# A softmax division that is placed later in the plan and held there

## The chip, the core and the metric

The kernel runs on one core of a Trainium2 chip. The metric is the device time of one execution in microseconds (us). The core has TensorE for matrix products (PE in the rows, PEld for its weight loads), VectorE (DVE), ScalarE (ACT), GpSimd (POOL) and SyncE (SP), which here only issues transfers. Each engine works through its own queue of instructions in order, and an instruction that waits holds those behind it.

## What is computed

Attention over 4 batches of 8 heads, 576 tokens and a head size of 64, with a decay from the running sum of log f and a causal mask. A gated MLP with a spatial mixing over tokens follows, and then a second MLP with a token shift.

```python
scores = scale * np.matmul(q, k.transpose(0, 1, 3, 2))
decay = cum[:, :, :, None] - cum[:, :, None, :]
scores = np.where(causal, -1000000000.0, scores + decay)
attn = np.exp(scores - np.max(scores, axis=-1, keepdims=True))
attn = attn / (np.sum(attn, axis=-1, keepdims=True) + 1e-09)
x = np.matmul(attn, v)               # then heads side by side: 576 x 512 per batch
h = np.maximum(x @ w_in, 0.0)        # u, v: its two halves; v normalized per token
gated = u * (np.einsum('ts,bsd->btd', w_spatial, v_n) + b_spatial[None, :, None])
x = gated @ w_out
k = np.maximum(xk @ w_k, 0.0)        # xk, xr: mixes of x and x one token earlier
out = sigmoid(xr @ w_r) * (k * k @ w_v)
```

## The kernel before

The 32 heads are taken in 16 pairs. Each head passes the same steps. q and k of a pair are scaled, split into two 16-bit halves on ScalarE and VectorE (`qkhi`, `qklo`), and turned by a transposing transfer. `score` and `rowmax` find the row maxima (tile nm); `mrow` splits them (nmh), turns them with a product and sends them through DRAM (md) into the rows of qA. `scoreT` computes the transposed scores and their exponentials e on ScalarE, `causal` masks e on POOL, and `pv` multiplies with v, which has a block of ones beside it, so that the sums of the softmax come out as rows of the same PSUM tile o. There is one such tile.

The division follows. `head` (L359) copies o to xo, which has three buffers, and sends the head's row of sums to DRAM (rd<-xo, L368). Once per pair, `recip` (L370) fetches both rows spread over 128 partitions (r<-rd, L375), adds the small constant, scales and inverts them on VectorE (L376, L377), sends them back (rd<-r, L378) and fetches them spread over 64 partitions for each head (sr<-rd, L381, two transfers). `norm` (L383) multiplies xo by sr on POOL, 64 partitions at a time, which gives x. `xhi` (L390) copies x to the high 16-bit half of xt on ScalarE, and `xlo` (L393) computes the low half on POOL. All these transfers are issued by SyncE, as are the loads of q, k and v, the transposing transfers, and those of md and qA.

The MLP of a batch starts with xt of its four pairs: `m1v` and `m1u` are the products with w_in, `ln1` to `ln4` the normalization (with short scalar steps on POOL, mv), `m2` the spatial product. Its pieces lie between the heads of the next batch, and those of the last batch behind the last head. The second MLP comes after that.

The order of all this is a written plan. Every step has a due time in units of heads: the dictionary `P` holds offsets from a head's number g or, for pairs, from 2p, and `plan_attention` (L611) adds each step with its time and a priority. `run` (L605) sorts by time and then by priority and calls the steps, which gives the program order. The framework's scheduler then orders each engine's instructions anew: by its own reckoning of times it takes the instruction that is ready, the earlier one in program order first. So an instruction can pass others on its engine that the scheduler takes to be still waiting. `pin` (L56) calls `keep_in_program_order`, which puts an instruction behind the one before it on the same engine in program order; the others remain free.

Due times that matter for the change, as offsets from the head or pair: transposed scores at 0 to 0.66 and masks 0.06 later, products with v at 1.0 and 1.3, `head` at 1.35, `mrow` at 2p - 0.65, halves of k and q at 2p - 4.25 and 2p - 3.95, copies into kA and qA at 2p - 3.6 and 2p - 3.5, the MLP of batch b from 8b + 10.7 over 7 heads.

Of the kernel before, what the change touches and what calls it, by code (L numbers as in the profile page):

```python
# [7 lines left out]
F32 = mybir.dt.float32  # L8
# [5 lines left out]
ALU = mybir.AluOpType  # L14
# [14 lines left out]


P = dict(load=-8.0, sq=-5.6, ss=-5.2, sc=-5.0, hik=-4.6, lok=-4.25, hiq=-4.2, loq=-3.95, aux=-3.6,
         s=-2.4, m=-0.65, t=0.0, pv=1.0, out=1.35, rc=1.4, nr=1.9, xs=2.2, xl=2.4, mlp=2.7, mlplen=7.0, vload=-5.0, vsq=-3.0,
         w1=-3.8, w0=1.0, wsp=4.6)


# [4 lines left out]
class K:  # L40
# [318 lines left out]
    def head(self, g):  # L359

        nc = self.nc
        o = self.o.pop(g)
        h = g % 2
        t = self.xo[h] = self.at.tile([128, 576], F32, tag="xo", bufs=3, name="xo")
        nc.scalar.copy(t, o[:, 256:832])
        if h == 0:
            self.rd = [self.hl.tile([2, 576], F32, tag=f"rd{i}", bufs=2, name=f"rd{i}") for i in range(2)]
        nc.sync.dma_start(self.rd[0][h:h + 1], t[64 - 64 * h:65 - 64 * h])  # L368

    def recip(self, p):  # L370

        nc = self.nc
        sv = self.sv[p // 4]
        r = self.at.tile([128, 9], F32, tag="r9", bufs=2, name="r9")
        nc.sync.dma_start(r, self.rd[0].rearrange("h (p c) -> (h p) c", c=9))  # L375
        nc.vector.tensor_scalar(r, r, 1e-9, sv[:, 1:2], op0=ALU.add, op1=ALU.mult)  # L376
        nc.vector.reciprocal(r, r)  # L377
        nc.sync.dma_start(self.rd[1].rearrange("h (p c) -> (h p) c", c=9), r)  # L378
        self.sr = self.at.tile([128, 576], F32, tag="sr", bufs=2, name="sr")
        for h in range(2):  # L380
            nc.sync.dma_start(self.sr[64 * h:64 * h + 64], self.rd[1][h:h + 1].to_broadcast([64, 576]))  # L381

    def norm(self, p):  # L383

        self.xp = self.at.tile([128, 576], F32, tag="x", bufs=2, name="x")
        for h in range(2):
            r = slice(64 * h, 64 * h + 64)
            self.nc.gpsimd.tensor_tensor(self.xp[r], self.xo[h][r], self.sr[r], ALU.mult)  # L388

    def xhi(self, p):  # L390
        self.nc.scalar.copy(self.xt[p % 8][:, 0, 0:576], self.xp)

    def xlo(self, p):  # L393
        t = self.xt[p % 8]
        self.nc.gpsimd.tensor_tensor(t[:, 1, 0:576], self.xp, t[:, 0, 0:576], ALU.subtract)

# [203 lines left out]
    def add(self, t, prio, fn, *args):  # L602
        self.steps.append((t, prio, len(self.steps), fn, args))
# [7 lines left out]
    def plan_attention(self):  # L611
        add, G = self.add, self.B * self.H
        for p in range(G // 2):
            T = 2.0 * p
            if p > 1:
                add(T + P["load"], 9, self.load, p, "k")
                add(T + P["load"] + 0.3, 9, self.load, p, "q")
            for i, nm in enumerate("kq"):
                add(T + P["sq"] + 0.1 * i, 2, self.qksq, p, nm)
            add(T + P["ss"], 2, self.qkscale, p)  # L620
            add(T + P["hik"], 2, self.qkhi, p, "k", "act")
            add(T - 4.2, 2, self.crow, p)
            add(T + P["lok"], 2, self.qklo, p, "k")
            add(T + P["hiq"], 2, self.qkhi, p, "q", "dve")
            add(T + P["loq"], 2, self.qklo, p, "q")
            add(T + P["aux"], 2, self.kaux, p)
            add(T + P["aux"] + 0.1, 2, self.qaux, p)
            for h in range(2):
                for u in range(4):
                    add(T + P["s"] + h + 0.22 * u, 4, self.score, 2 * p + h, u)  # L630
                    add(T + P["s"] + h + 0.22 * u + 0.05, 1, self.rowmax, 2 * p + h, u)
            add(T + P["m"], 0, self.mrow, p)
        for g in range(G):
            for u in range(4):
                add(g + P["t"] + 0.22 * u, 0, self.scoreT, g, u)
            for c, u in ((0, 0), (1, 1), (2, 2), (3, 2), (4, 3)):
                add(g + P["t"] + 0.22 * u + 0.06, 1, self.causal, g, c)
            for hf in range(2):
                add(g + P["pv"] + 0.3 * hf, 5, self.pv, g, hf)
            add(g + P["out"], 1, self.head, g)  # L640
            if g % 2:
                add(g + P["rc"], 1, self.recip, g // 2)
                add(g + P["nr"], 2, self.norm, g // 2)
                add(g + P["xs"], 2, self.xhi, g // 2)
                add(g + P["xl"], 2, self.xlo, g // 2)
        for b in range(self.B):
            for c in range(5):
                add(8 * b + P["vload"] + 0.2 * c if b else -3.2, 9, self.vload, b, c)
                add(8 * b + P["vsq"] + 0.3 * c, 3, self.vsq, b, c)
            add(8 * b + P["vsq"] + 1.8, 3, self.vscale, b)  # L650
# [222 lines left out]
```

## Time and profile before

| What | Before |
|---|---|
| Median of 3 runs | 751.19 us (749.28 to 755.62) |
| Profiled execution: span from first to last instruction | 750.9 us (no other time of this execution is shown) |
| Mean granted TensorE clock, as a share of full speed | 0.970 |
| Busy: TensorE, VectorE, ScalarE, POOL | 674.9, 426.8, 372.2, 184.5 us |
| Heads' copies out of PSUM, first and last start | 56.93 and 379.24 us |

The profile is of one execution. Busy times are unions of an engine's instructions; a busy TensorE isn't one at its peak, since its products are pipelined and their ends are modelled. A wait is idle time of an engine ahead of an instruction, put down to what ended last before it started. Which stretch a wait lies in decides what it costs: the heads are worked on until about 390 us, the last batch's first MLP until 445 us, and the second MLP to the end.

### The profile page before, as it was taken

To read this page: it belongs to the slowest core of one execution; us is meant where nothing else is said; L and a number is where in the kernel's file an instruction comes from. 1 tells how busy PE (TensorE), PEld (TensorE's weight loads), DVE (VectorE), ACT (ScalarE), POOL (GpSimd) and SP (SyncE) were. 2 spreads that over 40 slices of the span, in tenths; PEclk is the share of its full clock that TensorE was granted. 3 is DMA by queue.
4 is the path that set the end of the run, shared out by engine and by line. 5 is a ranking of instruction groups with operands and counts; after the bars stand their busy time and mean duration, and the time that the engine had idled before them with its cause. 6 is when DMAs were issued, how large, how long until landed. Compare 5 with 4: busy or idle time off the path is not lost.

```text
span 750.9 us, 11016 instructions
## 1 busy us (share of the span) xinstructions
PE 674.9 (90%) x3718; PEld 499.5 (67%) x3718; DVE 426.8 (57%) x1147; ACT 372.2 (50%) x740; POOL 184.5 (25%) x385
## 2 busy tenths in 40 slices
PE   0377878989998999999997679999999999999997
PEld 0245545647775677666774458788888888888886
DVE  5987786666655656646026879988225512632342
ACT  4626786666426854355505539747225412622431
POOL 7122645555324544445321201000000000000000
PEclk9998968999999999999999899999999999999999
DMA  9997666765655234410025453450100100010010
GB/s 228 203 204 158 168 138 131 147 137 107 126 133 122 56 71 99 97 27 18 18 64 184 146 192 124 140 164 15 42 27 16 57 0 15 1 56 1 1 57 28
DMA packets 130681, 69.78 MB, mean 93 GB/s; under 512 B 114704, under 2 KB 115312, under 8 KB 130624
## 3 DMA queue, kind: packets, MB, share of 16 engines
q1 hardware_dynamic: 128032, 67.89, 37.1%
q10 hardware_dynamic: 2592, 1.19, 0.7%
q8 instruction: 29, 0.48, 0.3%
q14 instruction: 28, 0.23, 0.1%
HBM read 42.06 MB, written 9.79 MB: 69 GB/s over the span
## 4 chain that ended last, share of the span: by engine, by line
PE 60%; DMA 16%; DVE 10%; POOL 5%; issue 3%; ACT 3%; SPq 1%; DVEq 0%; ACTq 0%; POOLq 0%
PE m L715 40%; PE o L357 7%; DMA sr<-rd 3%; POOL x L388 3%; PE m L575 3%; PE m1v L504 3%; PE s L302 3%; PE t L335 2%; PE m1u L558 2%; DMA rd<-r 2%; DVE junk L311 2%; DMA r<-rd 2%; DMA wst<-in_moe_w_k_dram 1%; DMA rd<-xo 1%; DMA wst<-in_moe_w_in_dram 1%
## 5 line engine op out<-in xcount | busy, mean ns | idle before, releaser
L357 PE MATMUL o<-e,v 128*128 128x320 f32 (+4 forms) x448 | 114.0, 384 | 5.5 <-POOL e L344 3.7
L715 PE MATMUL m<-xx,moe_w_k 128*128 128x512 f32 (+1 forms) x480 | 107.5, 373 | 0.4 <-ACT x L710 0.4
L715 PE MATMUL m<-moe_w_v,k 128*128 128x512 f32 x432 | 104.8, 391 | 0.0
L339 ACT ACTIVATE e<-t,qa 128x512 f32<-128x512 f32 (+1 forms) x128 | 72.6, 590 | 50.4 <-PE t L335 50.1
L311 DVE CUSTOM_DVE_ANT_0 junk<-s,mask 128x512 bf16<-128x512 f32 (+4 forms) x160 | 75.9, 474 | 37.8 <-PE s L302 32.2
L715 PEld LDWEIGHTS m<-xx,moe_w_k 128*128 128x128 f32 x480 | 84.0, 188 | 18.1 <-ACT x L710 0.9
L357 PEld LDWEIGHTS o<-e,v 128*128 128x128 f32 x448 | 78.5, 199 | 23.7 <-POOL e L344 6.1
L715 PEld LDWEIGHTS m<-moe_w_v,k 128*128 128x128 f32 x432 | 80.7, 188 | 17.7
L344 POOL TENSOR_SCALAR_AFFINE_SELECT e<-e 128x128 f32<-128x128 f32 (+1 forms) x160 | 52.2, 342 | 125.5 <-ACT e L339 123.0
L751 DVE TENSOR_TENSOR tmp<-tmp 128x512 f32<-128x512 f32 (+1 forms) x40 | 25.5, 638 | 88.1 <-ACT tmp L750 87.9
L302 PE MATMUL s<-kT,qT 128*128 128x512 f16 (+2 forms) x192 | 55.8, 299 | 21.6 <-DVE nm L311 13.7
L504 PE MATMUL m1v<-win,xt 128*128 128x512 f16 x240 | 61.5, 397 | 0.0
L388 POOL TENSOR_TENSOR x<-xo,sr 64x576 f32<-64x576 f32 x32 | 47.0, 1469 | 47.6 <-DMA sr<-rd 46.4
L715 PE MATMUL m<-gh,moe_w_out 128*128 128x512 f32 (+1 forms) x240 | 55.1, 380 | 3.5 <-DVE u L578 3.5
L335 PE MATMUL t<-qA,kA 69*128 69x512 f16 (+2 forms) x192 | 51.6, 294 | 7.3 <-DMA qA<-md 6.7
L558 PE MATMUL m1u<-xt,win 128*128 128x288 f16 x384 | 53.6, 286 | 4.5 <-ACT u L560 4.5
L750 ACT ACTIVATE tmp<-m 128x512 f32<-128x512 f32 (+1 forms) x40 | 22.1, 556 | 71.6 <-PE m L715 71.4
L575 PE MATMUL m<-wspT,vn 128*128 128x288 f16 x384 | 54.4, 290 | 3.0 <-DVE u L578 2.3
L302 PE MATMUL s<-kA,qA 67*128 67x512 f16 (+2 forms) x192 | 50.6, 300 | 4.0 <-DMA kA<-kT 3.7
L701 POOL COPY x<-x 128x4 f32<-128x4 f32 x4 | 3.5, 884 | 198.1 <-ACT x L710 198.1
L715 PEld LDWEIGHTS m<-gh,moe_w_out 128*128 128x128 f32 x240 | 43.3, 193 | 13.0 <-DVE u L578 3.8
L335 PE MATMUL t<-qT,kT 128*128 128x512 f16 (+2 forms) x192 | 51.4, 293 | 0.0
(159 smaller groups left out, 1083.8 us busy)
## 6 DMA issues: line engine op xcount, KB each, us to landing
sr<-rd SPq DMA_DIRECT2D x32, 144.0 KB
gd<-u SPq DMA_DIRECT2D x16, 288.0 KB
out_dram<-o SPq DMA_DIRECT2D x18, 256.0 KB
knat<-in_k_dram SPq DMA_DIRECT2D x32, 128.0 KB
v<-in_v_dram SPq DMA_DIRECT2D x32, 128.0 KB
g<-gd SPq DMA_DIRECT2D x16, 256.0 KB
wst<-in_moe_w_k_dram SPq DMA_DIRECT2D x8, 512.0 KB
wst<-in_moe_w_v_dram SPq DMA_DIRECT2D x8, 512.0 KB
```

What stands on the lines that cost most here:

```text
L302: self.nc.tensor.matmul(s[:, o:o + n], self.tok(qn, p, h, 128 * ib - 64, 128)[0:r], self.tok(kn, p, h, k0, n)[0:r], start=(j == 0), stop=( ...
L311: self.nc.vector.tensor_tensor_reduce(out=self.junk[r0:, 0:n], in0=self.s[u % 2][r0:, o:o + n], in1=self.mask[r0:, m0:m0 + n], op0=ALU.add ...
L335: self.nc.tensor.matmul(t[:, o:o + n], self.tok(kn, p, h, 128 * c, 128)[0:r], self.tok(qn, p, h, q0, n)[0:r], start=(j == 0), stop=(j == 1))
L339: self.nc.scalar.activation(self.e[g][:, 512 * u:512 * u + n], t[:, 0:n], AF.Exp, scale=self.qa[p][:, 5:6])
L344: self.nc.gpsimd.affine_select(out=e, in_=e, pattern=[[1, n]], compare_op=ALU.is_ge, fill=0.0, base=0, channel_multiplier=-1)
L357: self.nc.tensor.matmul(o[:, 256 + f:256 + q1], v[:, c, h // 2, 64 * (h % 2):64 * (h % 2) + 128], e[:, off:off + q1 - f], start=(c == 0), ...
L388: self.nc.gpsimd.tensor_tensor(self.xp[r], self.xo[h][r], self.sr[r], ALU.mult)
L504: nc.tensor.matmul(self.m1p, xt[:, xs, 128 * j:128 * j + 128], self.win[:, ws, kc, 512:1024], start=(kc == 0 and n == 0), stop=(kc == 3 an ...
L558: self.nc.tensor.matmul(o, self.win[:, ws, kc, fs], self.xt[(4 * b + kc) % 8][:, xs, ts_], start=(kc == 0 and n == 0), stop=(kc == 3 and n ...
L575: nc.tensor.matmul(o, pairs[n][0], pairs[n][1], start=(n == 0), stop=(n == 13))
L715: self.nc.tensor.matmul(out, l, r, start=(first and j == 0), stop=(last and j == len(pairs) - 1))
L751: nc.vector.tensor_tensor(tmp[:, 0:n], tmp[:, 0:n], tmp[:, 0:n], ALU.mult)
```

## The change

The division is cut into more steps, each with a due time of its own, and the instructions of all pairs but the last are pinned. `head` keeps the copy alone. The row of sums goes to DRAM in `denom` at g + 1.55 instead of 1.35 (heads 30 and 31 keep 1.35). From the number g of a pair's odd head: `sums` (r<-rd) at 1.8 instead of 1.4, `recip` at 2.1 instead of 1.4, `back` (rd<-r) at 2.25 instead of 1.4, `spread` (sr<-rd) at 2.5 instead of 1.4, `norm` at 2.9 instead of 1.9, `xhi` at 3.15 instead of 2.2, `xlo` at 3.2 instead of 2.4. The last pair keeps its old times and isn't pinned. The number of instructions, their shapes and all buffer counts stay as they were.

```diff
-        t = self.xo[h] = self.at.tile([128, 576], F32, tag="xo", bufs=3, name="xo")
+        t = self.xo[g] = self.at.tile([128, 576], F32, tag="xo", bufs=3, name="xo")
         nc.scalar.copy(t, o[:, 256:832])
+
+    def denom(self, g):
+
+        h = g % 2
         if h == 0:
             self.rd = [self.hl.tile([2, 576], F32, tag=f"rd{i}", bufs=2, name=f"rd{i}") for i in range(2)]
-        nc.sync.dma_start(self.rd[0][h:h + 1], t[64 - 64 * h:65 - 64 * h])
+        self.held(g // 2, self.nc.sync.dma_start(self.rd[0][h:h + 1], self.xo[g][64 - 64 * h:65 - 64 * h]))
+
+    def sums(self, p):
+
+        self.r9 = self.at.tile([128, 9], F32, tag="r9", bufs=2, name="r9")
+        self.held(p, self.nc.sync.dma_start(self.r9, self.rd[0].rearrange("h (p c) -> (h p) c", c=9)))
+        self.rdp = self.rd
+
+    def held(self, p, x):
+        if p < self.B * self.H // 2 - 1:
+            self.pin(x)
 
     def recip(self, p):
...
+        self.held(p, nc.vector.tensor_scalar(r, r, 1e-9, sv[:, 1:2], op0=ALU.add, op1=ALU.mult))
         nc.vector.reciprocal(r, r)
...
+    def back(self, p):
+
+        self.held(p, self.nc.sync.dma_start(self.rdp[1].rearrange("h (p c) -> (h p) c", c=9), self.r9))
+
+    def spread(self, p):
+
         self.sr = self.at.tile([128, 576], F32, tag="sr", bufs=2, name="sr")
         for h in range(2):
-            nc.sync.dma_start(self.sr[64 * h:64 * h + 64], self.rd[1][h:h + 1].to_broadcast([64, 576]))
+            self.held(p, self.nc.sync.dma_start(self.sr[64 * h:64 * h + 64], self.rdp[1][h:h + 1].to_broadcast([64, 576])))
...
-            self.nc.gpsimd.tensor_tensor(self.xp[r], self.xo[h][r], self.sr[r], ALU.mult)
+            self.held(p, self.nc.gpsimd.tensor_tensor(self.xp[r], self.xo.pop(2 * p + h)[r], self.sr[r], ALU.mult))
...
+        self.held(p, self.nc.scalar.copy(self.xt[p % 8][:, 0, 0:576], self.xp))
...
+        self.held(p, self.nc.gpsimd.tensor_tensor(t[:, 1, 0:576], self.xp, t[:, 0, 0:576], ALU.subtract))
...
             add(g + P["out"], 1, self.head, g)
+            add(g + (1.55 if g < G - 2 else P["out"]), 1, self.denom, g)
             if g % 2:
-                add(g + P["rc"], 1, self.recip, g // 2)
-                add(g + P["nr"], 2, self.norm, g // 2)
-                add(g + P["xs"], 2, self.xhi, g // 2)
-                add(g + P["xl"], 2, self.xlo, g // 2)
+                for fn, prio, x, y in ((self.sums, 1, 1.8, 1.4), (self.recip, 1, 2.1, 1.4), (self.back, 1, 2.25, 1.4), (self.spread, 1, 2.5, 1.4),
+                                       (self.norm, 2, 2.9, 1.9), (self.xhi, 2, 3.15, 2.2), (self.xlo, 2, 3.2, 2.4)):
+                    add(g + (x if g < G - 1 else y), prio, fn, g // 2)
```

## Rows read from the trace of the kernel before

**Rows 1.** Windows: stretch, length, busy us (instructions) per engine, PEclk, DMA, GB/s.

```profile
50.00:130.00 80.00, 66.44 (x349) 43.26 (x348) 59.91 (x223) 54.67 (x120) 38.62 (x73) 0.83 0.73 158
130.00:395.00 265.00, 255.66 (x1700) 175.39 (x1699) 138.09 (x461) 133.69 (x276) 117.27 (x238) 0.99 0.40 87
395.00:445.00 50.00, 34.04 (x237) 23.51 (x234) 37.73 (x74) 26.06 (x53) 7.90 (x25) 0.93 0.52 171
445.00:751.00 306.00, 301.66 (x1368) 247.71 (x1368) 152.03 (x275) 134.10 (x244) 3.54 (x4) 0.99 0.15 50
```

**Rows 2.** Waits, 40 to 395 us: who waited for whom, total us, times, longest.

```profile
POOL x L388 <- DMA sr<-rd: 46.4, 17, 11.7
ACT xt L391 <- POOL x L388: 37.5, 11, 10.9
...
DVE r L376 <- DMA r<-rd: 23.2, 9, 9.0
...
PE s L302 <- DVE nm L311: 11.0, 13, 3.3
...
PE t L335 <- DMA qA<-md: 6.7, 5, 2.5
PEld o L357 <- POOL e L344: 6.1, 6, 2.7
...
PE o L357 <- POOL e L344: 3.7, 2, 2.4
```

**Rows 3.** Waits of the transfer queue of SyncE, whole span.

```profile
SPq L368 <- ACT xo L365: 57.9, 15, 9.7
...
SPq L378 <- DVE r L377: 17.5, 11, 3.2
```

**Rows 4.** Timeline, 276 to 292 us, one pair: start, us, instruction, [idle before].

```profile
276.94 0.64 ACT L365 COPY xo<-o 128x576 f32<-128x576 f32 x1 [0.45 <-PE o L357]
...
278.75 0.35 SPq L375 DMA_DIRECT2D r<-rd  x1
280.94 0.34 SPq L378 DMA_DIRECT2D rd<-r  x1
282.40 1.11 SPq L381 DMA_DIRECT2D sr<-rd  x2
...
285.31 3.72 POOL L388 TENSOR_TENSOR x<-xo,sr 64x576 f32<-64x576 f32 x2 [1.85 <-DMA sr<-rd]
```

**Rows 5.** Timeline, 148 to 163 us.

```profile
152.30 1.40 POOL L388 TENSOR_TENSOR x<-xo,sr 64x576 f32<-64x576 f32 x1 [3.39 <-DMA sr<-rd]
...
153.73 0.64 ACT L365 COPY xo<-o 128x576 f32<-128x576 f32 x1 [2.93 <-POOL x L388]
...
156.93 2.07 DVE L534 TENSOR_SCALAR vt<-vt,mv 128x512 f32<-128x512 f32 x2 [5.88 <-POOL mv L529]
...
159.87 0.38 PE L302 MATMUL s<-kT,qT 128*128 128x512 f16 x1 [2.25 <-DVE nm L311]
```

**Rows 6.** Timeline, 209 to 233 us.

```profile
215.71 0.23 DVE L376 TENSOR_SCALAR r<-r,sv 128x9 f32<-128x9 f32 x1 [3.13 <-DMA r<-rd]
...
223.43 2.87 POOL L388 TENSOR_TENSOR x<-xo,sr 64x576 f32<-64x576 f32 x2 [4.23 <-DMA sr<-rd]
...
226.33 0.67 ACT L391 CAST xt<-x 128x576 f16<-128x576 f32 x1 [6.41 <-POOL x L388]
...
229.38 2.18 PE L357 MATMUL o<-e,v 128*128 128x320 f32 x6 [2.42 <-POOL e L344]
```

**Rows 7.** Timeline of ScalarE, 130 to 141 us.

```profile
139.35 0.64 ACT L365 COPY xo<-o 128x576 f32<-128x576 f32 x1
```

**Rows 8.** Timeline of VectorE and POOL, 88 to 104 us.

```profile
90.56 0.17 DVE L319 TENSOR_TENSOR nmh<-nm,nmh 128x10 f16<-128x10 f32 x1
...
100.29 2.87 POOL L388 TENSOR_TENSOR x<-xo,sr 64x576 f32<-64x576 f32 x2 [5.26 <-DMA sr<-rd]
...
100.43 1.28 DVE L319 TENSOR_TENSOR nmh<-nm,nmh 128x10 f16<-128x10 f32 x1
```

More of the change, by code (lines that the diff above doesn't have):

```diff
@@ L31 @@
 P = dict(load=-8.0, sq=-5.6, ss=-5.2, sc=-5.0, hik=-4.6, lok=-4.25, hiq=-4.2, loq=-3.95, aux=-3.6,
-         s=-2.4, m=-0.65, t=0.0, pv=1.0, out=1.35, rc=1.4, nr=1.9, xs=2.2, xl=2.4, mlp=2.7, mlplen=7.0, vload=-5.0, vsq=-3.0,
+         s=-2.4, m=-0.65, t=0.0, pv=1.0, out=1.35, mlp=2.7, mlplen=7.0, vload=-5.0, vsq=-3.0,
          w1=-3.8, w0=1.0, wsp=4.6)
@@ L373, in recip @@
         sv = self.sv[p // 4]
-        r = self.at.tile([128, 9], F32, tag="r9", bufs=2, name="r9")
-        nc.sync.dma_start(r, self.rd[0].rearrange("h (p c) -> (h p) c", c=9))
-        nc.vector.tensor_scalar(r, r, 1e-9, sv[:, 1:2], op0=ALU.add, op1=ALU.mult)
+        r = self.r9
+        self.held(p, nc.vector.tensor_scalar(r, r, 1e-9, sv[:, 1:2], op0=ALU.add, op1=ALU.mult))
         nc.vector.reciprocal(r, r)
-        nc.sync.dma_start(self.rd[1].rearrange("h (p c) -> (h p) c", c=9), r)
+    def back(self, p):
+        self.held(p, self.nc.sync.dma_start(self.rdp[1].rearrange("h (p c) -> (h p) c", c=9), self.r9))
+    def spread(self, p):
         self.sr = self.at.tile([128, 576], F32, tag="sr", bufs=2, name="sr")
         for h in range(2):
-            nc.sync.dma_start(self.sr[64 * h:64 * h + 64], self.rd[1][h:h + 1].to_broadcast([64, 576]))
+            self.held(p, self.nc.sync.dma_start(self.sr[64 * h:64 * h + 64], self.rdp[1][h:h + 1].to_broadcast([64, 576])))
     def norm(self, p):
@@ L387, in norm @@
             r = slice(64 * h, 64 * h + 64)
-            self.nc.gpsimd.tensor_tensor(self.xp[r], self.xo[h][r], self.sr[r], ALU.mult)
+            self.held(p, self.nc.gpsimd.tensor_tensor(self.xp[r], self.xo.pop(2 * p + h)[r], self.sr[r], ALU.mult))
     def xhi(self, p):
-        self.nc.scalar.copy(self.xt[p % 8][:, 0, 0:576], self.xp)
+        self.held(p, self.nc.scalar.copy(self.xt[p % 8][:, 0, 0:576], self.xp))
     def xlo(self, p):
         t = self.xt[p % 8]
-        self.nc.gpsimd.tensor_tensor(t[:, 1, 0:576], self.xp, t[:, 0, 0:576], ALU.subtract)
+        self.held(p, self.nc.gpsimd.tensor_tensor(t[:, 1, 0:576], self.xp, t[:, 0, 0:576], ALU.subtract))
     def weights1_setup(self):
```

## The prediction

> **What bounds the kernel now.** I began with the windows by stage. After 445 us TensorE is busy 301.66 of 306 us; nothing of the change is there. From 395 to 445 us it idles 16 us while the last MLP batch and the next weights are prepared. Heads are worked on before that: from 50 to 130 us TensorE is busy 66.44 of 80 us at a granted clock of 0.83, with VectorE busy 59.91; from 130 to 395 us it is busy 255.66 of 265 us at 0.99 [rows 1]. So the later stretch can give back at most 9.3 us of idle time and some 2.7 us of clock (0.01 x 265), and the early one 13.6 us of idle time and as much again of clock (0.17 x 80), if something other than TensorE's own work causes them.
>
> The waits come second. POOL stood 46.4 us before the halves of x until the spread sums landed, ScalarE 37.5 us before the copy to xt until POOL was done with x, VectorE 23.2 us before the reciprocal until the sums landed [rows 2]. On the transfer queue the row of sums waited 57.9 us for the copy out of PSUM, and the transfer after the reciprocal waited 17.5 us [rows 3]. Each such wait holds everything behind it on its engine. What TensorE itself paid is much smaller: 11.0 us for row maxima, 6.7 us for the maxima's transfer, 6.1 and 3.7 us for masked exponentials [rows 2], 27.5 us in all, of which only a part stems from these waits.
>
> Third, the timeline of one undisturbed pair gives the chain's length: copy at 276.94, four kinds of transfer one behind the other, the last issued at 282.40, x from 285.31 [rows 4]. That is 8.4 us, some 0.7 of a head: this copy and the one at 139.35 [rows 7] are twelve heads apart, 11.5 us each.
>
> Fourth, two places where it reaches TensorE. At 152.30 x had waited 3.39 us; behind it on POOL stood the layer norm's scalars, for which VectorE waited 5.88 us, and then the row maxima, for which TensorE waited 2.25 us. ScalarE's copy at 153.73 waited 2.93 us for that same x, because it needed one of the three xo buffers [rows 5]. At 215.71 VectorE had waited 3.13 us for the sums; at 223.43 x had waited 4.23 us, at 226.33 the copy to xt 6.41 us, and the next exponentials and their masks stood behind it, so that TensorE lost 2.42 us at 229.38 [rows 6].
>
> **The change, part by part.** No instruction is added or taken away. Per pair six transfers move on the transfer queue, two small instructions on VectorE, the two products and the low half on POOL, one copy on ScalarE. Their positions in the plan, from the odd head's number: row of sums 1.35 to 1.55, regrouping 1.4 to 1.8, reciprocal 1.4 to 2.1, return 1.4 to 2.25, spread 1.4 to 2.5, product 1.9 to 2.9, high half 2.2 to 3.15, low half 2.4 to 3.2. So copy to product is now 1.55 heads, some 18 us, where the transfers need 8.4 us: each wait should have ended when its instruction's turn comes, provided that the engines keep the plan's pace.
>
> What is returned. The two shown cases are 2.25 and 2.42 us, 4.7 us. Of what TensorE otherwise waited for row maxima, the maxima's transfer and masks (27.5 less 4.7, 22.8 us) I credit a quarter, 5.5 us: nine waits for sums held VectorE and fifteen for the copy held the transfer queue, but row maxima also wait on VectorE's other work, and a quarter lies nearer to the shown two than to all. Sum: **10 us**. Bounds: nothing, if TensorE only idles elsewhere; all 27.5 us and some of the early clock at the other end. The clock is left out of the sum, since a stall returned early may be lost again in the same stretch.
>
> What stays. The last pair isn't held and keeps its place: the longest waits of POOL and of ScalarE, 11.7 and 10.9 us [rows 2], are that pair's and remain. The two products still fill POOL for 2.87 us a pair [rows 6].
>
> What is late next. (1) The return transfer now sits at 1.25 of a two-head cycle, just ahead of the maxima's two transfers at 1.35, and is held there. Its waits for the reciprocal averaged 1.6 us (17.5 over 11) [rows 3]. The maxima are first needed 0.65 heads later, some 7 us, and the undisturbed chain shows 1.5 to 2.2 us from one issue to the next [rows 4], so two transfers leave some 2.6 us of cover: cost nothing; uncovered, 15 x 1.6 = 24 us. (2) The MLP of a batch is planned from 10.7 heads after its first; x of its last pair comes at 10.2 instead of 9.4. That leaves half a head, some 6 us: cost nothing; if x missed it, one wait of a row's size, 2 to 4 us, in each of three batches. (3) The xo buffers, under the rivals.
>
> TensorE 750.9 - 10 = 740.9, taken as **741 us**. The sum is made against the profiled execution's span of 750.9 us, the only time shown of that execution; the median of the three runs is 751.19 us, so no shift is made.
>
> **Rivals.** *No change* (B). The hold is only against the instruction before in the plan; that one may itself be ordered early, by a reckoning in which transfers land sooner than in the trace. Then the same waits stand behind other instructions. Or TensorE, busy 255.66 of 265 us, was the bound in the long stretch all along. For it: 46.4 us of POOL's wait correspond to under 10 us of TensorE's masks waits. Against it: rows 6 show the way from wait to TensorE without a break. Time 748 to 753, say 751 us.
>
> *The xo buffers* (C), the one that ends slower. A pair's product frees the buffer that the copy three heads after its even head needs. That copy is planned at 4.35 from the even head, the product was at 2.9 and is now at 3.9: of 1.45 heads of margin 0.45 is left, some 5 us. Even with the old margin it ran out once by 2.93 us, when the copy followed the one two heads earlier (139.35 us) by only 14.4 us [rows 5, 7]. While ScalarE waits, no exponential starts. At 2.9 us a time, the forecast's 10 us are used up by the fourth pair; with six of 15 pairs it is slower by over 1%. I price it at seven: 741 + 20 = 761 us. Against it: the product now stands behind the masks of the very head whose copy would wait, so this copy still has that head's whole product with v before it.
>
> *The lock* (D). A VectorE operation with two SBUF inputs took 1.28 us at 100.43, under the product on POOL from 100.29, and 0.17 us at 90.56 [rows 8]; its work was stretched by 1.1 us. The products move from beside the row-maximum split (1.35 in the cycle) to beside the splits of k and q (1.75 and 2.05), which also take two SBUF inputs. Three POOL instructions a pair at 1.1 us are 3.3 us; past 130 us VectorE, busy 138 of 265, hides them, and the splits are due 1.6 heads before use. If the early stretch, with VectorE busy 59.91 of 80, doesn't hide them, five pairs cost 16 us: 757 us. The Trainium skill ("SBUF — State Buffer", section Who interferes with whom) states the rule: two engines share one port pair, a VectorE instruction with two SBUF inputs and a GpSimd instruction that reads SBUF exclude each other, and whoever starts second waits for the whole of the other. The two rows agree with it. By that rule alone, each product of about 1.4 us could hold one split.
>
> *More than forecast* (E). If three quarters of the 22.8 us come back instead of a quarter, the saving is 4.7 + 17 = 22 us: 729 us.
>
> **How the numbers follow.** About 1%, 7.5 us, is what a measurement of this kernel can tell from no change. Forecast (A) 0.50, its own range 734 to 747: 0.38 of it is faster by over 1%, 0.12 within 1%. B 0.22, all within. C 0.15: 0.14 slower, 0.01 within. D 0.05: 0.03 slower, 0.02 within. E 0.08, faster. Sums: faster 0.46, within 1% 0.37, slower 0.17. Predicted 741 us. The range of 730 to 757 takes in A and B whole, D up to its price and the near side of E, and leaves out most of C.
>
> **What would show it.** In the changed kernel's profile POOL's wait for the spread sums should fall from 46.4 us to under 20 (11.7 of it the last pair's), VectorE's for the sums from 23.2 to under 8, ScalarE's for x from 37.5 to under 20, the queue's for the copy from 57.9 to under 25. From 130 to 395 us the same heads should end 5 to 8 us sooner, from 50 to 130 us some 3 us. The step from these waits to TensorE is wrong if they fall and the last head's copy comes no sooner. B shows as the same waits in new places, C as ScalarE's copies waiting for x in six or more pairs, D as splits of 1.4 us or more beside the products. The whole is wrong if the stretch from 395 to 445 us, which is left untouched, moves by more than the forecast's 10 us.

## The result, and the profile after

The changed kernel takes **755.66 us** (median of 20 runs, 751.49 to 763.23) against 751.36 us for the kernel before beside it (20 runs, 746.93 to 755.62): ratio 1.0061, 95% interval 1.0041 to 1.0080. I had forecast 741 us. A second series gave 756.91 us and 1.0056 (1.0031 to 1.0081). The profile below is of that second series, since the first one fell on a disturbed execution; its span is 755.1 us.

First the windows of the changed kernel that answer to [rows 1], in the same columns.

```profile
50.00:130.00 80.00, 63.76 (x338) 41.18 (x337) 59.80 (x224) 53.33 (x118) 34.01 (x71) 0.87 0.77 157
130.00:395.00 265.00, 252.14 (x1665) 175.24 (x1664) 137.42 (x460) 132.99 (x278) 116.45 (x239) 0.98 0.38 86
395.00:445.00 50.00, 41.96 (x276) 28.58 (x275) 35.43 (x71) 24.89 (x51) 10.83 (x28) 0.90 0.50 163
```

Fixed windows compare different work once one kernel is ahead. So I cut both executions at the same events: first copy out of PSUM, ninth copy (head 8), last copy, first product of the second MLP. First the kernel before, then the changed one.

```profile
56.90:131.10 74.20, 60.93 (x320) 39.78 (x318) 55.76 (x208) 52.08 (x116) 34.56 (x61) 0.82 0.69 149
131.10:379.20 248.10, 238.76 (x1583) 163.75 (x1582) 133.53 (x452) 131.71 (x272) 112.53 (x234) 0.99 0.41 88
379.20:444.90 65.70, 49.74 (x348) 34.24 (x345) 41.21 (x82) 27.27 (x55) 11.97 (x28) 0.95 0.45 149
```

```profile
60.50:142.30 81.80, 63.09 (x339) 40.80 (x337) 62.76 (x223) 55.32 (x123) 35.99 (x65) 0.85 0.73 147
142.30:386.10 243.80, 234.16 (x1562) 163.58 (x1561) 125.81 (x437) 126.34 (x266) 108.59 (x229) 0.99 0.37 84
386.10:449.00 62.90, 52.30 (x349) 35.56 (x346) 41.16 (x83) 27.15 (x55) 11.75 (x29) 0.92 0.48 155
```

Here the result comes apart. The long stretch is 4.3 us shorter (243.80 against 248.10) and the tail to the second MLP 2.8 us (62.90 against 65.70), but the ninth copy comes 11.2 us later. Of these, 3.6 us lie ahead of the first copy. That copy starts between 57.2 and 60.5 us in the versions below and follows no pattern that I could find, so these 3.6 us stay open. The other 7.6 us lie in the first eight heads, where TensorE idles 18.7 us (81.80 less 63.09) against 13.3. The net is +4.1 us. Everything behind the second MLP's first product takes 306 us in both.

The 7.6 us can be placed more closely. From the copy of head 4 to that of head 8, first before, then changed:

```profile
92.30:131.10 38.80, 31.56 (x159) 20.22 (x157) 28.76 (x123) 28.35 (x67) 18.82 (x31) 0.78 0.65 133
96.50:142.30 45.80, 34.48 (x175) 21.87 (x175) 35.06 (x132) 30.95 (x72) 20.21 (x36) 0.81 0.68 136
```

That is 7.0 us of the 7.6.

The waits between 40 and 400 us, to set beside [rows 2], and those of SP's queue in that stretch, beside [rows 3]: total us, times, longest. The window ends 5 us later than in [rows 2], so that the last pair is still inside it here, as it is there.

```profile
POOL x L407 <- DMA sr<-rd: 61.8, 14, 8.0
...
ACT xo L365 <- POOL x L407: 29.9, 7, 8.2
ACT xt L410 <- POOL x L407: 26.0, 8, 11.1
...
DVE r L389 <- DMA r<-rd: 14.1, 4, 11.8
```

```profile
SPq L372 <- ACT xo L365: 47.4, 14, 8.0
SPq L394 <- DVE nmh L319: 16.1, 2, 12.0
SPq L394 <- DVE r L390: 10.3, 6, 2.6
```

POOL waits longer for the spread sums, not shorter, and seven of ScalarE's copies wait 29.9 us for a free xo buffer, where it had been 3.4 us in 2. That was my rival C to the number of places, and the first theory I tested. It turned out to be the right ring and the wrong places: of the seven waits only one, of 1.86 us, lies in the first eight heads, where the loss is.

The place that pays is visible in the timeline of SP, TensorE, POOL and ScalarE in heads 3 to 7 (L502 is the transposing transfer of the spatial weights, wspT; start, us, instruction, wait before it).

```profile
106.39 1.30 SPq L502 DMA_TRANSPOSE wspT<-n  x1
107.73 1.38 SPq L400 DMA_DIRECT2D sr<-rd  x2
109.15 0.44 SPq L372 DMA_DIRECT2D rd<-xo  x1
109.76 1.39 SPq L502 DMA_TRANSPOSE wspT<-n  x1
114.97 0.30 SPq L325 DMA_DIRECT2D md<-mr  x1
...
121.19 2.91 SPq L502 DMA_TRANSPOSE wspT<-n  x2
124.16 0.72 SPq L377 DMA_DIRECT2D r<-rd  x1
```

```profile
99.94 1.27 PE L357 MATMUL o<-e,v 128*128 128x320 f32 x6
...
111.10 2.92 POOL L407 TENSOR_TENSOR x<-xo,sr 64x576 f32<-64x576 f32 x2 [1.02 <-DMA sr<-rd]
...
114.09 0.64 ACT L365 COPY xo<-o 128x576 f32<-128x576 f32 x1
...
125.08 1.19 PE L357 MATMUL o<-e,v 128*128 128x320 f32 x6
...
135.15 2.88 POOL L407 TENSOR_TENSOR x<-xo,sr 64x576 f32<-64x576 f32 x2
136.58 0.64 ACT L365 COPY xo<-o 128x576 f32<-128x576 f32 x1 [1.86 <-POOL x L407]
```

Head 5's products with v are done at 101.21 (99.94 + 1.27), yet its copy starts at 114.09, 12.9 us later. It needs the buffer of head 2, which the first half of the second pair's x frees at about 112.5 us. That x starts at 111.10, because its spread transfer was issued at 107.73, directly behind the first transpose of the spatial weights. No wait for x is recorded ahead of this copy: ScalarE has other work for most of that time, and the scheduler has put the copy behind it, I take it because it reckons with the buffers too. So a list of waits doesn't show this delay at all. That the buffer decides it is shown below, where a fourth one brings the copy to 101.10.

Head 7's products are done at 126.27 and its copy starts at 136.58, 10.3 us later, the moment the first half of the third pair's x has freed the buffer. That pair's regrouping (r<-rd) was issued at 124.16, directly behind the third and fourth of these transposes. (It also needs the sums of head 5, whose transfer left only at 116.69. But with the fourth buffer, where head 5 is early, it still leaves at 123.27, again behind these two transposes.) There is one PSUM tile o, so no further product with v starts in either time. In the kernel before, the spread goes ahead of all the transposes and the regrouping ahead of the third, and the copies come sooner:

```profile
97.03 1.31 SPq L381 DMA_DIRECT2D sr<-rd  x2
...
104.26 2.92 SPq L483 DMA_TRANSPOSE wspT<-n  x2
...
109.60 0.35 SPq L375 DMA_DIRECT2D r<-rd  x1
```

```profile
103.76 0.61 ACT L365 COPY xo<-o 128x576 f32<-128x576 f32 x1
...
122.20 0.64 ACT L365 COPY xo<-o 128x576 f32<-128x576 f32 x1 [0.45 <-POOL x L388]
```

The regrouping at 109.60 leaves behind the first two transposes; the third and fourth come after it, at 115.63 and 118.57.

### The profile page after: what moved, and what is told of

Read it like the earlier page. It is cut to its first block, busy times and chain, and to the rows that moved or that the text cites. A ratio compares the mean times of both kernels' runs of the same rounds, so it can differ in the third digit from the quotient of the medians.

```text
span 761.5 us, 11012 instructions
## 1 busy us (share of the span) xinstructions
PE 681.2 (89%) x3718; PEld 504.6 (66%) x3718; DVE 424.2 (56%) x1147; ACT 369.8 (49%) x740; POOL 182.4 (24%) x385
## 4 chain that ended last, share of the span: by engine, by line
PE 60%; DMA 14%; DVE 10%; POOL 5%; ACT 5%; issue 3%; SPq 2%; DVEq 0%; ACTq 0%; POOLq 0%
PE m L734 40%; PE o L357 6%; PE m L594 4%; PE s L302 3%; PE m1u L577 3%; PE t L335 3%; DMA sr<-rd 3%; DMA md<-mr 2%; POOL x L407 2%; DMA knat<-in_k_dram 2%; DMA qT<-nq 2%; DMA wst<-in_moe_w_k_dram 2%; DVE junk L311 2%; DMA qA<-qT 1%; PE m1v L523 1%
## 5 line engine op out<-in xcount | busy, mean ns | idle before, releaser
L734 PE MATMUL m<-moe_w_v,k 128*128 128x512 f32 x432 | 104.8, 391 | 0.0
L357 PEld LDWEIGHTS o<-e,v 128*128 128x128 f32 x448 | 81.9, 206 | 20.8 <-issue 3.9
L302 PE MATMUL s<-kT,qT 128*128 128x512 f16 (+2 forms) x192 | 56.6, 305 | 24.9 <-DVE nm L311 12.9
L302 PE MATMUL s<-kA,qA 67*128 67x512 f16 (+2 forms) x192 | 52.2, 310 | 7.9 <-DMA qA<-qT 4.3
```

The lines of the kernel that those rows point to most:

```text
L302: self.nc.tensor.matmul(s[:, o:o + n], self.tok(qn, p, h, 128 * ib - 64, 128)[0:r], self.tok(kn, p, h, k0, n)[0:r], start=(j == 0), stop=( ...
L357: self.nc.tensor.matmul(o[:, 256 + f:256 + q1], v[:, c, h // 2, 64 * (h % 2):64 * (h % 2) + 128], e[:, off:off + q1 - f], start=(c == 0), ...
L734: self.nc.tensor.matmul(out, l, r, start=(first and j == 0), stop=(last and j == len(pairs) - 1))
```

## The experiments

Each run has the kernel before beside it on the same chip; ratios are to that, with 95% intervals. Two numbers from each profile place a run: the ninth copy, and the length from there to the last copy (the long stretch). Where a fence shows part of a line, only that part was changed.

**First set: the ring, the pin, the time.** Theory then: the pinned spread waits behind qA<-md, x comes late, and the three xo buffers turn that into the loss.

Spread ahead of qA<-md (2.3 instead of 2.5):

```diff
- (self.spread, 1, 2.5, 1.4)
+ (self.spread, 1, 2.3, 1.4)
```

> The changed kernel, with the spread transfers due at 2.3 instead of 2.5, so that the instruction ahead of them in the plan is the return transfer and no longer the transfer of the maxima into qA. In the changed kernel 4 to 10 transfers, with the transposing ones and qA<-md among them, stand between rd<-r and sr<-rd in seven pairs in the built queue; here 0 to 3, and qA<-md in none. Theory 1 (the spread is held behind qA<-md, so x is late, the three xo buffers run out and ScalarE's copies wait): POOL's wait for sr falls from 54 us (40 to 400 us) to under 30, ScalarE's waits of xo for x from 29.0 us to under 6, and the time from 755.7 to 744 to 750 us. Theory 2 (a later x is bad in itself, whatever holds it): the time stays at 754 to 758 us. Theory 3 (any new order moves the time by some us, and 0.6% is that): the time lies anywhere in 748 to 758 us and does not follow the waits.

Measured 750.59 us, 0.9965 (0.9937 to 0.9993). Ring waits of ScalarE fell to 9.8 us in 3, POOL's for sr to 32.6 us: the waits moved as meant, though not under the bounds named, and 0.96% came back, just short of the forecast. At 2.3 the second pair's spread is due ahead of the first transpose as well, so this run doesn't tell qA<-md from the transposes.

Four xo buffers, paid for with one x buffer:

```diff
-        t = self.xo[g] = self.at.tile([128, 576], F32, tag="xo", bufs=3, name="xo")
+        t = self.xo[g] = self.at.tile([128, 576], F32, tag="xo", bufs=4, name="xo")
...
-        self.xp = self.at.tile([128, 576], F32, tag="x", bufs=2, name="x")
+        self.xp = self.at.tile([128, 576], F32, tag="x", bufs=1, name="x")
```

> The changed kernel with four xo buffers instead of three, and one buffer for x instead of two to make room. The queue of transfers keeps the spread behind qA<-md in seven pairs. Theory 1: POOL's wait for sr stays at 45 to 60 us, but ScalarE's waits of xo for x go to 0 to 2 us; since the copies are what reaches the exponentials and TensorE, most of the loss comes back: 747 to 752 us. If the loss goes through POOL's queue (masks and scalars behind x) and not through the buffers, the time stays at 753 to 757 us with the xo waits gone. Theory 2: 754 to 758 us. Theory 3: anywhere in 748 to 758 us.

Measured 746.09 us, 0.9922 (0.9891 to 0.9953). The spread is as late as ever (issued at 108.04, x at 111.46), but head 5's copy starts at 101.10 instead of 114.09. The length from the ninth to the last copy is 243.3 us, against 243.8 with three buffers: in the long stretch the ring cost nothing that can be seen.

Late times without pins, and pins at the old times:

```diff
-        if p < self.B * self.H // 2 - 1:
+        if False:
```

> The changed kernel without any hold: the later due times alone, every instruction free again. In the built queue at most two transfers stand between rd<-r and sr<-rd and qA<-md never. Theory 1: no spread behind qA<-md, so ScalarE's xo waits are under 6 us and the time is 745 to 751 us; POOL's wait for sr is near the 46 us of the kernel before, because free instructions go as early as before. Theory 2: due times are what costs, so 754 to 758 us. Theory 3: anywhere in 748 to 758 us.

Measured 761.13 us, 1.0127 (1.0093 to 1.0161); the waits of [rows 2] are back (POOL 52.8 us, the copy to xt 42.2 us, between 40 and 405 us), the long stretch takes 253.7 us. All three theories had it faster.

```diff
-            add(g + (1.55 if g < G - 2 else P["out"]), 1, self.denom, g)
+            add(g + P["out"], 1, self.denom, g)
...
-                    add(g + (x if g < G - 1 else y), prio, fn, g // 2)
+                    add(g + y, prio, fn, g // 2)
```

> The changed kernel with all due times of the kernel before, the instructions of 15 pairs held all the same: the hold alone. In the built queue qA<-md stands between rd<-r and sr<-rd in two early pairs. Theory 1: the hold is harmless where the instruction ahead is early, so the waits are as before (POOL for sr 40 to 50 us, xo for x under 6 us) and the time is 748 to 753 us. If the hold in itself costs (it takes freedom from the scheduler), 754 to 758 us. Theory 3: anywhere in 748 to 758 us.

Measured 757.96 us, 1.0073 (1.0046 to 1.0101), long stretch 248.1 us, outside what the first theory named. Neither half alone shortens the long stretch; both together do.

**Second set: four buffers elsewhere, and edits that don't touch the division.** The kernel before with four xo buffers and one x buffer, and the version with the spread at 2.3 with them:

> The kernel before with four xo buffers instead of three and one x buffer instead of two: the same room as in the changed kernel with four, without the change. Theory 1: before, ScalarE waits only 3.4 us for x on account of xo, so at most 3 us come back: 748 to 752 us, against 746.1 us for the change with four buffers; the later places would then be worth something once the buffers no longer run out. If the buffers alone make the gain of that kernel, 744 to 748 us. Theory 3 (a new order by itself moves the time by 0.5 to 1%): anywhere in 744 to 760 us.

> The changed kernel with both remedies: the spread due at 2.3, ahead of qA<-md, and four xo buffers with one x buffer. Theory 1: both sides of the loss are gone, so POOL's wait for sr is about 33 us, the xo waits under 2 us, and the time is at or under that of the better single remedy: 742 to 748 us. Theory 3: anywhere in 744 to 760 us, so that the two remedies do not add.

Measured 759.23 us, 1.0079 (1.0049 to 1.0109), and 749.28 us, 0.9951 (0.9926 to 0.9976). Both missed what the first theory named. The exchange of buffers made the kernel before slower, so it isn't good in itself, and the 1.4% that it brings the changed kernel (0.9922 against 1.0061) comes from the ring that was short there. With the spread at 2.3, where the ring was hardly short, it brought nothing (0.9951 against 0.9965). How much of each figure is only another order, the next two runs bound.

How far does the order scatter with edits that have nothing to do with the division?

```diff
-         w1=-3.8, w0=1.0, wsp=4.6)
+         w1=-3.8, w0=1.0, wsp=4.5)
```

> A control: the kernel before with the eight steps that prepare the spatial weights due 0.1 head earlier (4.5 instead of 4.6). Nothing of the division is touched; the scheduler writes another order from there on (1759 lines of difference on TensorE). Theories 1 and 2 expect the time of before within 0.3%: 749 to 755 us. Theory 3 expects a shift of 4 to 9 us either way.

```diff
- vsq=-3.0
+ vsq=-2.9
```

> A second control: the kernel before with the sums of squares of v due 0.1 head later (-2.9 instead of -3.0). Nothing of the division is touched; the order differs in 1949 lines on TensorE. Theories 1 and 2: 749 to 755 us. Theory 3: a shift of 4 to 9 us either way, and not the same one as in the first control.

Measured 757.12 us, 1.0048 (1.0026 to 1.0070), and 753.36 us, 1.0002 (0.9986 to 1.0019). A tenth of a head in the spatial weights' time alone costs half a per cent. The two numbers scatter as well: in these two controls the ninth copy stands at 134.8 and 136.7 us (131.1 in the kernel before) and the long stretch takes 252.5 and 243.6 us (248.2). A loss of 0.6% could therefore be scatter, and needed more than one version on either side.

**Third set: the changed kernel with such an edit.** The changed kernel again, then with wsp at 4.5, then this with the spread at 2.3, and the changed kernel with only the spread unpinned:

> The changed kernel once more, beside the kernel before, for a second profile of it. 755 to 758 us, ratio 1.004 to 1.009. Theory 1: ScalarE's waits of xo for x are again about seven, 20 to 30 us together, on another execution; if they were an accident of the first profile they are under 8 us.

> The changed kernel with the control's edit on top (spatial weights due 0.1 head earlier): another order, and the spread still behind qA<-md in as many pairs. Theory 1: the xo waits stay at 20 to 35 us and the time at 753 to 762 us, slower than before. Theory 3: the loss of the changed kernel belongs to one order alone, so this one lies anywhere in 745 to 762 us.

> The changed kernel with the spread ahead of qA<-md (2.3) and the control's edit on top: another order, no spread behind qA<-md. Theory 1: xo waits under 12 us and 745 to 752 us, at or under the kernel before and clearly under the same edit without the moved spread. Theory 3: anywhere in 745 to 762 us, no steady distance to the run with the spread behind.

```diff
-            self.held(p, self.nc.sync.dma_start(self.sr[64 * h:64 * h + 64], self.rdp[1][h:h + 1].to_broadcast([64, 576])))
+            self.nc.sync.dma_start(self.sr[64 * h:64 * h + 64], self.rdp[1][h:h + 1].to_broadcast([64, 576]))
```

> The changed kernel with the hold taken off the spread alone; its due time stays 2.5, all other holds stay. In the built queue 0 to 3 transfers stand between rd<-r and sr<-rd, qA<-md never. Theory 1: as with the spread due at 2.3: xo waits under 12 us, 745 to 752 us. Theory 3: anywhere in 745 to 762 us.

Measured 756.91 us, 1.0056 (1.0031 to 1.0081); 750.37 us, 0.9964 (0.9941 to 0.9987); 746.20 us, 0.9919 (0.9895 to 0.9944); 746.96 us, 0.9927 (0.9901 to 0.9952). The second of these felled the first theory: the same ring waits (27.0 us in 6, and 71.5 us of POOL's wait), and yet faster than the kernel before. Cutting all profiles at the same events suggested why. From the ninth to the last copy, the versions so far that are late and pinned take 238.8 to 243.8 us, the others (the kernel before, its controls, times without pins, pins without times, the kernel before with four buffers) 243.6 to 253.7. The two ranges touch: the control with vsq moved is as short as the changed kernel. But as a group the late and pinned versions had the gain, and what differed among them was the ninth copy, from 134 to 142 us, against 131 in the kernel before.

**Fourth set: where along the heads.** The change in the last twelve pairs alone, in the first four alone, and the first with the spread unpinned:

```diff
-        if p < self.B * self.H // 2 - 1:
+        if 4 <= p < self.B * self.H // 2 - 1:
...
-            add(g + (1.55 if g < G - 2 else P["out"]), 1, self.denom, g)
+            add(g + (1.55 if 8 <= g < G - 2 else P["out"]), 1, self.denom, g)
...
-                    add(g + (x if g < G - 1 else y), prio, fn, g // 2)
+                    add(g + (x if 8 <= g < G - 1 else y), prio, fn, g // 2)
```

In the second version the three conditions read `p < 4`, `g < 8` and `g < 8`; the third version adds the unpinned spread shown above.

> The later times and the pins for the last twelve pairs alone (heads 8 to 31); the first four pairs keep the times of the kernel before and no pin. Theory now (the long stretch gains what was forecast, 4 to 10 us from the ninth copy to the second MLP, and the loss lies in the order of the first eight heads): ninth copy at 131 to 136 us into the span as in the kernel before (131.1), last copy 239 to 244 us later, run at 742 to 748 us, ratio 0.985 to 0.995. Rival (what is lost hangs on the later heads: the buffer ring of xo, with 7 waits of 29.9 us): ninth copy early as well, but the time at 755 us or more, ratio 1.00 to 1.01. Rival (the place of the ninth copy scatters with any edit and has nothing to do with the first eight heads' own times): ninth copy anywhere from 134 to 140, ratio 0.99 to 1.00.

> The later times and the pins for the first four pairs alone (heads 0 to 7); the last twelve pairs keep the times of the kernel before and no pin. Theory now: ninth copy late, at 138 to 146 us into the span, then a stretch as long as in the kernel before (246 to 252 us to the last copy): 757 to 764 us, ratio 1.006 to 1.015, slower than the whole change. Rival (the ring of xo in the later heads): little changed, 750 to 754 us, ratio 0.997 to 1.003. Rival (scatter of the early order): ninth copy at 134 to 140, ratio 1.00 to 1.008.

> As the version with the last twelve pairs late and pinned, and in these the two sr<-rd transfers have their late time but no pin, so that they are not tied behind qA<-md. Theory now: the gain of the early order and that of the freed transfers add up; waits of POOL for sr about 33 us between 40 and 405 us, ring waits of xo under 10 us, 740 to 746 us, ratio 0.982 to 0.990. Rival (freeing the transfers alone was what helped in its twin, the early order scatters): ratio 0.990 to 0.995, as the whole change without that pin (0.9927).

Measured 742.27 us, 0.9861 (0.9832 to 0.9891); 766.24 us, 1.0185 (1.0152 to 1.0217); 740.86 us, 0.9845 (0.9814 to 0.9877), not to be told from the first. The second lost somewhat more than its theory named. The halves add up: -9.5 and +14.5 us against 751.77 us make +5.0, and the whole change is +4.3. Windows of the first two, cut at the same events:

```profile
57.90:133.20 75.30, 60.70 (x318) 39.66 (x317) 57.60 (x210) 51.79 (x115) 33.83 (x61) 0.80 0.70 149
133.20:375.00 241.80, 234.95 (x1582) 164.36 (x1580) 129.90 (x449) 129.45 (x273) 110.82 (x233) 0.99 0.41 89
375.00:435.40 60.40, 50.93 (x349) 34.98 (x346) 39.23 (x80) 26.72 (x54) 12.22 (x29) 0.94 0.47 153
```

```profile
59.50:143.60 84.10, 66.96 (x338) 42.94 (x337) 62.19 (x224) 55.09 (x123) 35.56 (x65) 0.80 0.70 147
143.60:391.60 248.00, 234.81 (x1564) 161.66 (x1563) 128.53 (x435) 128.19 (x266) 109.87 (x229) 0.99 0.37 81
```

The first keeps the early stretch of the kernel before (75.30 us, against 74.20) and the gain of the long one; the second has the long stretch of the kernel before (248.00) and the loss. The waits of the first, between 40 and 395 us:

```profile
POOL x L407 <- DMA sr<-rd: 56.2, 14, 7.9
...
ACT xo L365 <- POOL x L407: 20.0, 5, 8.4
```

It is 1.4% faster than the kernel before with more of both waits. Sums of waits did not tell what the change was worth.

**Fifth set: which part costs it in the first eight heads.** The whole change, with other pins in the first four pairs: none; those of the engines alone; those of SP's transfers alone.

```diff
-    def held(self, p, x):
-        if p < self.B * self.H // 2 - 1:
+    def held(self, p, x, sp=0):
+        if p < self.B * self.H // 2 - 1 and (p >= 4 or not sp):
```

That is the second of them; `sp=1` is passed for the four kinds of transfers. The third has `p >= 4 or sp`, the first `4 <= p` alone.

> The whole change with its later times for all sixteen pairs, but the first four pairs carry no pin. Beside it stand the version with the first four pairs left as before (742.3 us) and the whole change (756). Theory (the pins on SP's transfers hold up the transposes and weight loads of the first eight heads): ninth copy at 131 to 137 us, 742 to 749 us, ratio 0.985 to 0.995. Rival (the later times themselves cost it there): ninth copy at 139 to 144 us, 752 to 758 us, ratio 1.00 to 1.007. Rival (scatter): in between, 748 to 752 us.

> The whole change, but in the first four pairs only the steps on DVE, ACT and POOL are pinned, and the four kinds of transfers on SP (rd<-xo, r<-rd, rd<-r, sr<-rd) are not. Theory (SP's pins): 742 to 749 us, ratio 0.985 to 0.995, the spatial weights' load no later than 86 us into the span (83.0 before, 88.7 in the changed kernel). Rival (the pins on the engines): 752 to 758 us, ratio 1.00 to 1.007. Rival (the later times): the same 752 to 758 us, and then the version without pins there is slow too.

> The whole change, but in the first four pairs only the transfers on SP are pinned, and the steps on DVE, ACT and POOL are not. Theory (SP's pins): as slow as the whole change, 752 to 758 us, ratio 1.00 to 1.007, ninth copy at 139 to 144 us. Rival (the pins on the engines): 742 to 749 us, ratio 0.985 to 0.995. Rival (the later times): 752 to 758 us, as with every set of pins.

Measured 745.89 us, 0.9897 (0.9863 to 0.9931); 746.48 us, 0.9910 (0.9878 to 0.9942); 756.01 us, 1.0044 (1.0017 to 1.0070). The loss follows the pins on SP's queue: it is gone without them and back with them alone. The later times and the pins on the engines cost at most 0.5% in these heads (0.9897 and 0.9910 against 0.9861 for the version that leaves the first four pairs alone, with intervals that overlap). (The long stretch takes 243.4, 242.2 and 246.3 us.) Which of the four kinds of transfers it is was not run kind by kind; the timeline points to the second pair's spread and the third pair's regrouping. One detail of what I expected missed: the spatial weights' load wasn't earlier without SP's pins (87.84 us). What was earlier is the division itself. The version with the engines' pins alone, same events as above:

```profile
97.67 1.28 SPq L400 DMA_DIRECT2D sr<-rd  x2
...
105.15 2.91 SPq L502 DMA_TRANSPOSE wspT<-n  x2
...
110.20 0.35 SPq L377 DMA_DIRECT2D r<-rd  x1
...
112.75 1.37 SPq L502 DMA_TRANSPOSE wspT<-n  x1
...
115.02 1.38 SPq L502 DMA_TRANSPOSE wspT<-n  x1
```

```profile
101.03 2.90 POOL L407 TENSOR_TENSOR x<-xo,sr 64x576 f32<-64x576 f32 x2 [7.46 <-DMA sr<-rd]
...
103.31 0.62 ACT L365 COPY xo<-o 128x576 f32<-128x576 f32 x1
...
128.92 0.33 PE L357 MATMUL o<-e,v 128*128 128x64 f32 x2
129.28 0.64 ACT L365 COPY xo<-o 128x576 f32<-128x576 f32 x1 [0.73 <-PE o L357]
```

The spread passes the transposes here and the regrouping the last three of them, the copy of head 5 starts 10.8 us sooner, and that of head 7 follows its own last product (128.92 + 0.33) instead of x. All versions in the order of the first column, those with a fourth xo buffer at the end (us; sr is that of the second pair, r that of the third; the ratio is to the kernel before of the same series):

| Version | sr issued | copy, head 5 | r<-rd issued | copy, head 7 | ninth copy | ninth to last | ratio |
|---|---|---|---|---|---|---|---|
| before, wsp 4.5 | 95.8 | 102.5 | 108.5 | 126.3 | 134.8 | 252.5 | 1.0048 |
| late from head 8 | 96.4 | 103.2 | 109.0 | 121.3 | 133.2 | 241.7 | 0.9861 |
| before | 97.0 | 103.8 | 109.6 | 122.2 | 131.1 | 248.2 | 1 |
| early pins on engines only | 97.7 | 103.3 | 110.2 | 129.3 | 134.3 | 242.2 | 0.9910 |
| early, no pins | 97.7 | 103.3 | 111.0 | 131.1 | 135.8 | 243.4 | 0.9897 |
| late times, no pins at all | 97.9 | 103.6 | 110.8 | 131.4 | 136.1 | 253.7 | 1.0127 |
| before, vsq -2.9 | 98.1 | 104.8 | 110.7 | 128.4 | 136.7 | 243.6 | 1.0002 |
| late from head 8, spread unpinned | 98.3 | 105.1 | 110.7 | 122.8 | 131.7 | 243.3 | 0.9845 |
| wsp 4.5, spread at 2.3 | 99.3 | 104.5 | 118.3 | 130.3 | 134.3 | 241.1 | 0.9919 |
| pins at the old times | 100.0 | 104.7 | 112.0 | 128.6 | 135.3 | 248.1 | 1.0073 |
| spread at 2.3 | 100.1 | 106.3 | 121.0 | 131.6 | 138.1 | 243.8 | 0.9965 |
| spread unpinned | 101.5 | 106.5 | 122.5 | 132.2 | 139.1 | 238.8 | 0.9927 |
| wsp 4.5 | 104.2 | 109.0 | 121.4 | 132.2 | 136.0 | 242.4 | 0.9964 |
| early pins on SP only | 105.3 | 111.6 | 121.7 | 134.0 | 139.6 | 246.3 | 1.0044 |
| changed | 107.7 | 114.1 | 124.2 | 136.6 | 142.3 | 243.8 | 1.0056 |
| first eight heads only | 107.9 | 114.4 | 124.3 | 136.6 | 143.6 | 248.0 | 1.0185 |
| before, four xo buffers | 97.7 | 98.4 | 102.3 | 130.6 | 139.5 | 245.6 | 1.0079 |
| spread at 2.3, four xo buffers | 101.1 | 102.4 | 123.9 | 126.6 | 134.8 | 242.9 | 0.9951 |
| four xo buffers | 108.0 | 101.1 | 123.3 | 127.6 | 135.9 | 243.3 | 0.9922 |

With three buffers the copy of head 5 follows the issue of sr by 4.7 to 6.8 us; with a fourth it no longer does. The rest is looser. With three buffers and free transfers in the first eight heads the ninth copy stands anywhere from 131.1 to 136.7 us, so only some 6 us of the changed kernel's 11.2 stand out from what the order alone does. The time doesn't follow the ninth copy alone either, since the long stretch has its own share.

## Why the prediction was wrong

**The step that failed** is "what is late next". It asked what the held transfers would wait behind on SP's queue and named only the two of the maxima. It left out the five transposes of the spatial weights. In the plan they stand from 5.4 heads on, 0.4 apart, so the first is 0.1 ahead of the second pair's spread (5.5) and the fourth 0.2 ahead of the third pair's regrouping (6.8; 6.4 before). These weights are prepared by VectorE, ScalarE and POOL in the crowded first stretch and were late; unpinned, the division's transfers passed them, pinned they could not. So the spread left at 107.73 us instead of 97.03 (4.1 us of it were there at this pair's regrouping already, 95.63 against 91.55) and the third pair's regrouping at 124.16 instead of 109.60. SP's pins in the first four pairs alone keep the loss (1.0044), and without them it is gone (0.9910). With it fell "from 50 to 130 us some 3 us" sooner.

**Rival C** had the mechanism and seven waits, but not the price. I put every ring wait on the path at 2.9 us. In the long stretch they cost nothing that can be seen (243.8 us with three buffers, 243.3 with four, where one x buffer less was the price; 241.7 us in the version late from head 8, with five waits of 20.0 us). In heads 5 and 7 the short ring was worth most of the loss, since the fourth buffer takes the ninth copy from 142.3 to 135.9 us, and head 5 isn't even among the seven waits. My argument against C, that the copy which waits still has its own head's product ahead of it, is contradicted there by 12.9 and 10.3 us between last product and copy. Why the ring shows in one stretch and not in the other wasn't tried by itself. A guess: the pieces of the first MLP are planned from 10.7 on, and its first product starts at 128.67 us in the changed kernel, so that while head 5's copy is late TensorE has no such work to turn to, and later it has.

**The saving** was right in size and wrong in its way. Where the whole change is left out of the first four pairs, the kernel takes 742.27 us, against 741 forecast (746.48 where only SP's pins are left out there). But POOL's wait, which should have fallen below 20 us, is 56.2 us there and 61.8 us in the changed kernel. VectorE's wait (14.1 us, not below 8) and ScalarE's for x (26.0 and 22.0, not below 20) fell less than forecast, and the queue's for the copy hardly (47.4, not below 25). None of the four signs came. So "rows 6 show the way from wait to TensorE" carried the number by luck: two cases were read, and the credit of a quarter was a choice. The 27.5 us that it was taken from also count some waits twice: the one at 229.38 stands in the rows as 2.42 us of TensorE's products and again as 2.73 us of its weight loads. Of the 9.1 us between the two spans (750.9 and 741.8), 6.3 lie between ninth and last copy: 2.5 us less TensorE idle time (9.3 against 6.9 us) and 3.8 us less busy time for the same count of products (1583 and 1582). Another 5.3 us lie in the stretch behind the last copy, which I had said would stay; the ninth copy 2.1 us later takes some back. Which instruction's place brought the 6.3 us stays open: times without pins and pins without times both fail to, and the control with vsq moved shows that a change of order alone can shorten this stretch by 4.6 us (243.6 against 248.2).

**The other items.** The return transfer of (1) did wait longer where it is held: 40.1 us in 13 waits, all its rows together, against 21.7 in 14 before. The largest row names VectorE's split of the maxima (L319) for 16.1 us in 2. That is a misnomer: in the case of 12.0 us the transfer left right behind the reciprocal that it carries, and before that split.

```profile
359.13 0.21 DVE L390 RECIPROCAL r<-r 128x9 f32<-128x9 f32 x1
...
359.37 0.34 SPq L394 DMA_DIRECT2D rd<-r  x1
359.41 0.17 DVE L319 TENSOR_TENSOR nmh<-nm,nmh 128x10 f16<-128x10 f32 x1
```

So it is the wait that (1) named, of the reciprocal's place on VectorE, beyond the 2.6 us of cover. TensorE's waits for the maxima's transfer fell all the same in the changed kernel (2.4 us in 3, against 6.7 in 5), but are 4.0 to 10.1 us in the versions with other pins or none in the first eight heads, so no run prices it. Of (2), the MLP found x late once, for 3.6 us in the profile of the changed kernel. No version had to be explained by the lock of rival D.

**The hold's reach.** Rival B's sentence, that the hold is only against the instruction before in the plan, was the right key, read for the wrong sign: I asked what happens if that instruction is early, and it was late. With wsp at 4.5 the second pair's spread is no longer behind the first transpose (issued at 104.2, the transpose at 106.0), and 0.9% of 756.91 us came back without a touch on the division, while the same edit cost the kernel before 0.5%.

## What to carry to other kernels

Before pinning an instruction, look up what stands directly ahead of it in program order on its queue, in every phase of the program and not in one steady-state cycle: the pin inherits that instruction's lateness, and a ring of buffers hands it on to the engine that matters. Cut two traces at the same events before comparing them, since windows of equal time and sums of waits hid both the gain and the loss here: a copy that the scheduler has put behind other work is late without a recorded wait. Where a neutral edit moves the time by 0.5%, judge a change by several versions on each side.

## What the runs showed of the hardware

A product on POOL stretched VectorE instructions of a few elements, too. The rows are of VectorE in the changed kernel; x was computed on POOL from 111.10 to 114.02.

```profile
111.05 0.16 DVE L79 TENSOR_SCALAR qa<-qa 128x2 int32<-128x2 int32 x1
111.12 0.15 DVE L496 TENSOR_TENSOR wb<-wb,n 128x1 f32<-128x1 f32 x1
...
111.26 1.30 DVE L81 TENSOR_SCALAR qa<-qa 128x2 int32<-128x2 int32 x1
...
112.67 1.37 DVE L496 TENSOR_TENSOR wb<-wb,n 128x1 f32<-128x1 f32 x1
```

L496 has two inputs from SBUF and took 0.15 us as x began, and 1.37 us under its second half, like the pair in [rows 8]. L81 has one input of the same shape as L79, and took 1.30 us where L79 took 0.16; it lies on the way to the scaling of the next q and k, for which ScalarE waited 1.82 us here, in a stretch where VectorE is busy 59.80 of 80 us. The Trainium skill ("SBUF — State Buffer", section Who interferes with whom) puts VectorE instructions with two SBUF inputs and those in a two-port mode under an exclusive lock with GpSimd; the two times of L496 agree; whether L81 ran in such a mode no run here shows.
